# Sketched attention into a squared-ReLU network: the numerators of two groups by single heads on row halves of the TensorE array

## The chip, the core and the metric

The kernel runs on one core of a Trainium2 chip. The metric is the device time of one execution in microseconds; the number compared is the median over several executions. A profiled execution gives the trace, whose clock starts with the program's first instruction (its span).

## What is computed

Four batches with four heads each, 1088 tokens, 32 elements to a head. Queries and keys are sketched: two 8x32 matrices S1 and S2 are applied, and all 64 products of their results are the features. Each head's numerator and denominator come from one 64x33 state (64 features by 32 values and a column of ones). What all four heads give a token (128 numbers) goes through a two-layer network with a squared ReLU between the layers.

```python
def phi(x):
    a = np.einsum('rd,bhsd->bhsr', S1, x)
    b = np.einsum('rd,bhsd->bhsr', S2, x)
    return np.einsum('bhsi,bhsj->bhsij', a, b).reshape(*x.shape[:-1], r * r)
q_p, k_p = (phi(q), phi(k))
kv = np.einsum('bhsf,bhsd->bhfd', k_p, v)
z = np.sum(k_p, axis=2)
num = np.einsum('bhsf,bhfd->bhsd', q_p, kv)
den = np.einsum('bhsf,bhf->bhs', q_p, z)[..., None] + 1e-06
...
h = x @ w_in
r = np.maximum(h, 0.0)
g = r * r
return (g @ w_out).astype(np.float32)
```

## The kernel before

The program is a list of operations, recorded by `attention(b)` for four batches and `ffn(n, ...)` for nine stretches of 384 or 512 tokens. A table written out by hand, PLAN, gives the one order in which all of them are issued, the engine of each, and which buffer each takes. Nothing is reordered when it runs: each engine takes its instructions in that order and waits on semaphores. The result buffers in PSUM are three of two banks (h0, h1, h2), one bank a0 and one bank o0.

An entry such as `num3.0:PE:h1` is the numerator of batch 3, group 0, on TensorE into h1. For each batch the operations around the change are:

- `ksk`, `ka`, `kp` (L371, L376, L384): the features of the keys.
- `kv` (L400): the state of four heads, 72 pairs of weight load and matmul in the trace, contraction over 128 tokens, 64 columns of weights, 33 columns moved. Heads 0 and 2 write partitions 0 to 63 of one bank, heads 1 and 3 partitions 64 to 127.
- `kve` (L413): copies of the state into SBUF. `kvz[b]` is 128 x 2 x 2 x 33: for each pair of heads a block diagonal, head 0 of the pair in partitions 0 to 63 with zeros beside it, head 1 in partitions 64 to 127.
- `qp`: the features of the queries, 128 partitions (two heads of 64) x 2 pairs x 1088 tokens. In batches 0 and 1 TensorE makes them (L435) in products of 32 rows and 64 columns of weights, and VectorE multiplies (L452). In batches 2 and 3 they are read back through DRAM, and VectorE multiplies (L501).
- `num` (L535): the numerators. A group of up to 24 blocks of 32 tokens is `nx` times four blocks. For each of these, each pair of heads and each two blocks there is one float32 matmul: weights are 128 rows x 64 tokens of `qp`, and 66 columns of `kvz` move, so that a pair's two heads come out side by side and the zeros keep them apart. Batches 2 and 3 have two groups each: group 0 with nx = 6 (24 matmuls) into an h buffer, group 1 with nx = 3 into a0.
- `mxa` (L550 on ScalarE, L552 on VectorE): the denominators out of PSUM. `mx` (L557, L558): the reciprocal, and the quotient into `xs`, both VectorE.
- `tx` (L571) and `xe` (L576): transposes on TensorE, and the copy into xT, from which the network reads.

For the network, `m1.n.m` (L601) is two matmuls of 512 columns, `r` (L613 on ScalarE, L615 on VectorE) the ReLU out of h, `g` (L626, L628) the square of two of these, `m2` (L636) eight matmuls into o0, and `oe` (L643) the copy out. The h buffers turn over between `m1`, `r` and the attention: `num2.0` takes h0 after `r.3.0` on VectorE has read it. On TensorE the order around the two groups is `m1.2.7 num2.0 m1.3.7 m2.2.5 m2.2.6 m2.2.7 m1.3.2 tx2.0 kv3.0` and `num2.1 num3.0 tx2.1 m2.4.0 m1.5.0 m1.5.6`.

In the trace each float32 matmul shows as two records, each with its weight load.

Of the kernel before, what the change touches and what calls it, by code (L numbers as in the profile page):

```python
# [23 lines left out]
N_AA = 3  # L24
N_HEAT = 24
NUM_M = (64, 64, 64, 64)
W_PARTS = ((0, 1), (1, 2), (2, 4))
MODE = ('pe', 'pe', 'dma', 'dma')
Q_LOADS = (((0, 8), (8, 34)), ((0, 34),), ((0, 34),), ((0, 34),))
# [77 lines left out]
def kernel(  # L107
# [11 lines left out]
    nc = tc.nc  # L119
    B, H, S, D = q.shape  # L120
# [15 lines left out]
    def T(name, shape, dt=F32):  # L136
        return sb.tile(shape, dt, name=name, tag=name)
# [24 lines left out]
    def at(buf):  # L162
        return tiles[buf.slot]
# [23 lines left out]
    kvz = [T(f"kvz{i}", [128, 2, 2, D + 1]) for i in range(B)]  # L187
    kvs = [T(f"kvs{i}", [128, 2, 2, D + 1]) if MODE[i] == "pe" else None for i in range(B)]
    qp = [T(f"qp{i}", [128, 2, S]) for i in range(2)]
# [6 lines left out]
    def add(name, engines, fn, deps=(), alloc=(), uses=(), n=0, after=()):  # L196
        op = Op(name, engines, fn, deps, alloc, uses, n, after)
        ops.append(op)
        return op
# [5 lines left out]
    for x, src in ((0, S1), (1, S2)):  # L205
        def f(e, x=x, src=src):
            en = {"SP": nc.sync, "ACT": nc.scalar}[e]
            en.dma_start(out=S_sb[R * x : R * x + R, :], in_=src)
# [21 lines left out]
    def STx():  # L230
        return at(stb)[:, 0 : 2 * R].rearrange("p (x r) -> p x r", x=2)
    o_SK = add("SK", "DVE", lambda e: nc.vector.tensor_tensor(
        out=SK, in0=STx()[:, :, None, :].to_broadcast([128, 2, H, R]),
# [37 lines left out]
    o_gate = add("gate", "POOL", lambda e: nc.gpsimd.tensor_copy(gate, kin[0][:, S - 1 : S]), n=1)  # L271
    for lo, hi_ in W_PARTS:
        def f(e, lo=lo, hi_=hi_):
# [7 lines left out]
    def wpart(ct):  # L281
        return [i for i, (lo, hi_) in enumerate(W_PARTS) if lo <= ct // 4 < hi_][0]

# [6 lines left out]
    def attention(b):  # L290
        i = b % 2
# [3 lines left out]
        def mine(key, op):  # L295
            hist.setdefault((b, key), []).append(op)
            return op
# [210 lines left out]
        for g, (c0, c1) in enumerate(QG):  # L508
            nx = (c1 - c0 + 3) // 4
            pb = 2 if nx == 4 else 3  # L510
            nb, tb, db = Buf("h") if nx > 3 else Buf("a", "h"), Buf("a", "h"), Buf("den")

            def f_num(e, c0=c0, c1=c1, nx=nx, nb=nb, pb=pb):
                for x in range(nx):
                    lo = 512 * (x // pb) + 132 * (x % pb)
                    t = at(nb)[:, lo : lo + 132].rearrange(
                        "p (m d) -> p m d", d=33)
                    cs = []
                    for cc in range(4):
                        c = c0 + 4 * x + cc  # L520
                        c = c if c < c1 else c - 2
                        cs.append((c, mode == "pe" and 2 * (c - c0) >= c1 - c0))
                    runs = []
                    for cc, (c, sw) in enumerate(cs):
                        if runs and runs[-1][3] == sw and runs[-1][1] + runs[-1][2] == c:
                            runs[-1][2] += 1
                        else:
                            runs.append([cc, c, 1, sw])
                    if len(runs) > 1 or NUM_M[b] < 128:
                        two = all(cs[2 * z][0] + 1 == cs[2 * z + 1][0] and cs[2 * z][1] == cs[2 * z + 1][1] for z in range(2))  # L530
                        w = 2 if two and NUM_M[b] > 32 else 1
                        runs = [[cc, cs[cc][0], w, cs[cc][1]] for cc in range(0, 4, w)]
                    for pr in range(2):
                        for cc, c, w, sw in runs:
                            nc.tensor.matmul(  # L535
                                t[32 * cc : 32 * cc + 32 * w, 2 * pr : 2 * pr + 2, :],
                                qp[i][:, pr, 32 * c : 32 * c + 32 * w], (kvs if sw else kvz)[b][:, pr],
                                start=True, stop=True)
            o_num = mine("num", add(f"num{b}.{g}", "PE", f_num, o_qp[g] + o_kve, alloc=[nb], n=nx))

            def views(nx=nx, nb=nb, db=db, pb=pb):
                k_, m_ = (2, 4 * pb) if nx > 3 else (1, 4 * nx)
                t = at(nb).rearrange("p (b s) -> p b s", b=1 if nb.slot[0] == "a" else 2)[:, 0:k_, 0 : 33 * m_]
                return k_, m_, t.rearrange("p b (m d) -> p b m d", d=33), *at(db)

            def f_mxa(e, views=views):
                k_, m_, t, den, rec, xs = views()
                dd = den[:, 0 : k_ * m_].rearrange("p (b m) -> p b m", b=k_)
                if e == "ACT":
                    nc.scalar.activation(dd, t[:, :, :, D], ACTF.Copy, bias=eps)  # L550
                else:
                    nc.vector.tensor_scalar_add(dd, t[:, :, :, D], eps)  # L552
            o_mxa = add(f"mxa{b}.{g}", "DVE|ACT", f_mxa, [o_num], alloc=[db], uses=[nb], n=4 * nx)

            def f_mx(e, views=views, nx=nx):
                k_, m_, t, den, rec, xs = views()
                nc.vector.reciprocal(rec[:, 0 : k_ * m_], den[:, 0 : k_ * m_])  # L557
                nc.vector.tensor_tensor(  # L558
                    out=xs[:, 0:nx].rearrange("p (b x) (h d) -> p b (x h) d", b=k_, d=D), in0=t[:, :, :, 0:D],
                    in1=rec[:, 0 : k_ * m_].rearrange("p (b m) -> p b m", b=k_)[:, :, :, None].to_broadcast([128, k_, m_, D]),  # L560
                    op=ALU.mult)
            assert nx in (1, 2, 3, 4, 6)
            o_mx = add(f"mx{b}.{g}", "DVE", f_mx, [o_mxa], uses=[nb, db], n=nx)
            cols = 32 * (c1 - c0)

            def f_tx(e, tb=tb, db=db, cols=cols, nx=nx):
                t = at(tb).bitcast(BF16)
                xs = at(db)[2]
                for x in range(nx):
                    n = min(128, cols - 128 * x)  # L570
                    nc.tensor.transpose(t[:, 128 * x : 128 * x + n], xs[0:n, x, :], ident[0:n, 0:n])  # L571
            o_tx = add(f"tx{b}.{g}", "PE", f_tx, [o_mx, o_id], alloc=[tb], uses=[db], n=nx)

            def f_xe(e, t0=S * b + 32 * c0, tb=tb, cols=cols):
                fn = nc.scalar.copy if e == "ACT" else nc.vector.tensor_copy
                fn(xT[:, t0 : t0 + cols], at(tb).bitcast(BF16)[:, 0:cols])  # L576
            o_xe = add(f"xe{b}.{g}", "ACT|DVE", f_xe, [o_tx], uses=[tb], n=cols)
            x_ops.append((S * b + 32 * c0, S * b + 32 * c1, o_xe))
# [82 lines left out]
    for b in range(B):  # L661
        attention(b)
# [52 lines left out]
```

## Time and profile before

| what | us |
|---|---|
| runs shown | 118.04 and 119.79, median 118.92 |
| profiled execution | 116.81 |
| its span | 114.9 |
| TensorE busy | 107.0 (93%) |
| VectorE busy | 96.5 (84%) |
| ScalarE busy | 82.5 (72%) |

The profiled execution took 116.81 us, of which the span from the first to the last instruction is 114.9; the granted clock of TensorE is 0.999. A row of a timeline has the start and the length in microseconds, the engine (PE is TensorE's matmuls, PEld its weight loads, DVE VectorE, ACT ScalarE), the line, the operation with its tiles, the part of the array (rows*columns), shapes, and how many records were merged; in brackets stands the idle time before it. Matmuls overlap, so a merged row's length is from its first start to its last end.

### The profile page before, as it was taken

To read this page: it belongs to the slowest core of one execution; us is meant where nothing else is said; L and a number is where in the kernel's file an instruction comes from. 1 tells how busy PE (TensorE), PEld (TensorE's weight loads), DVE (VectorE), ACT (ScalarE), POOL (GpSimd) and SP (SyncE) were. 2 spreads that over 40 slices of the span, in tenths; PEclk is the share of its full clock that TensorE was granted. 3 is DMA by queue.
4 is the path that set the end of the run, shared out by engine and by line. 5 is a ranking of instruction groups with operands and counts; after the bars stand their busy time and mean duration, and the time that the engine had idled before them with its cause. 6 is when DMAs were issued, how large, how long until landed. Compare 5 with 4: busy or idle time off the path is not lost.

```text
span 114.9 us, 4029 instructions
## 1 busy us (share of the span) xinstructions
PE 107.0 (93%) x1716; PEld 77.4 (67%) x1716; DVE 96.5 (84%) x137; ACT 82.5 (72%) x114; POOL 10.5 (9%) x40
## 2 busy tenths in 40 slices
PE   5999997899999999999979999999999999999940
PEld 2346584667866766787768768877757877788730
DVE  1679998499596999999599689989999999999920
ACT  3134614285885899999992769998799798998910
POOL 4050540630000420000000000000000000000000
PEclk9999999999999999999999999999999999999999
DMA  2999899689699572376696126124200002022412
GB/s 60 323 296 239 269 321 183 122 229 195 169 261 232 142 218 108 83 164 156 148 176 141 41 71 183 34 69 140 82 0 13 10 6 69 0 67 72 115 38 59
DMA packets 10129, 15.23 MB, mean 133 GB/s; under 512 B 2112, under 2 KB 6976, under 8 KB 10112
## 3 DMA queue, kind: packets, MB, share of 16 engines
q1 hardware_dynamic: 8864, 13.80, 45.2%
q0 software_dynamic: 992, 1.05, 5.9%
q8 instruction: 13, 0.21, 0.8%
q10 hardware_dynamic: 256, 0.13, 0.5%
q14 instruction: 4, 0.03, 0.1%
HBM read 13.24 MB, written 2.79 MB: 139 GB/s over the span
## 4 chain that ended last, share of the span: by engine, by line
PE 75%; DVE 13%; ACT 4%; issue 3%; DVEq 0%; ACTq 0%
PE o L636 26%; PE h L601 25%; PE h L535 5%; PE o L263 4%; PE a L400 4%; DVE qp L452 3%; DVE qT L421 2%; DVE kp L384 2%; PE h L400 2%; PE h L435 2%; PE h L464 2%; PE a L535 2%; ACT r L613 1%; DVE xs L558 1%; PE h L371 1%
## 5 line engine op out<-in xcount | busy, mean ns | idle before, releaser
L613 ACT ACTIVATE r<-h 128x1024 bf16<-128x1024 f32 (+1 forms) x54 | 50.5, 979 | 8.9 <-PE h L601 7.9
L636 PEld LDWEIGHTS <-g 128*128 128x128 bf16 x544 | 32.6, 98 | 7.6 <-DVE g L628 1.5
L601 PE MATMUL h<-xT,w_in 128*128 128x512 bf16 (+1 forms) x144 | 37.1, 369 | 0.3
L636 PE MATMUL o<-w_out,g 128*128 128x128 bf16 x544 | 36.5, 219 | 0.1
L628 DVE TENSOR_TENSOR g<-r 128x2048 bf16<-128x2048 bf16 (+1 forms) x35 | 32.9, 969 | 0.8 <-ACT r L613 0.2
L615 DVE TENSOR_SCALAR r<-h 128x1024 bf16<-128x1024 f32 (+1 forms) x18 | 20.7, 1160 | 1.3 <-PE h L601 0.9
L601 PEld LDWEIGHTS <-w_in 128*128 128x128 bf16 x144 | 13.7, 115 | 6.0 <-issue 0.4
L626 ACT ACTIVATE g<-r 128x2048 bf16<-128x2048 bf16 (+1 forms) x9 | 14.0, 1556 | 0.7 <-DVE r L615 0.5
L447 ACT COPY A<-h 128x256 f32<-128x256 f32 (+2 forms) x12 | 5.0, 464 | 7.3 <-PE h L435 7.3
L263 PE MATMUL o<-zero 128*128 128x512 bf16 x24 | 8.1, 474 | 1.2 <-DVE zero L202 1.2
L384 DVE TENSOR_TENSOR kp<-a,ka 128x1280 f32<-128x1280 f32 (+1 forms) x5 | 6.9, 1370 | 0.0
L452 DVE TENSOR_TENSOR qp<-h,A 128x256 f32<-128x256 f32 (+2 forms) x12 | 6.0, 517 | 0.9 <-ACT A L447 0.8
L435 PE MATMUL h<-qT,SR 32*64 32x128 f32 (+2 forms) x192 | 6.2, 325 | 0.0
L535 PEld LDWEIGHTS h<-kvz,qp 128*64 128x64 f32 x136 | 4.4, 137 | 2.5 <-issue 1.1
L535 PE MATMUL h<-kvz,qp 128*64 128x66 f32 x136 | 5.0, 224 | 0.7 <-issue 0.6
L421 DVE STREAM_TRANSPOSE qT<-qin 128x1088 f32<-128x1088 f32 (+2 forms) x5 | 5.4, 1080 | 0.2 <-DMA qin<-in_q_dram 0.2
L435 PEld LDWEIGHTS h<-qT,SR 32*64 32x64 f32 x192 | 3.6, 131 | 2.6 <-issue 0.8
L643 ACT COPY osb<-o 128x512 f32<-128x512 f32 (+1 forms) x7 | 3.9, 561 | 1.9 <-PE o L636 1.8
L263 PEld LDWEIGHTS <-zero 128*128 128x128 bf16 x24 | 2.2, 110 | 4.4 <-issue 2.2
L501 DVE TENSOR_TENSOR qp<-qp,Bq 128x1536 f32<-128x1536 f32 (+1 forms) x4 | 5.1, 1283 | 0.0
L353 DVE STREAM_TRANSPOSE kT<-kin 128x1024 f32<-128x1024 f32 (+1 forms) x5 | 5.1, 1019 | 0.0
L400 PEld LDWEIGHTS a<-vp,kp 128*64 128x64 f32 x144 | 4.4, 138 | 0.9 <-issue 0.8
(69 smaller groups left out, 93.4 us busy)
## 6 DMA issues: line engine op xcount, KB each, us to landing
vin<-in_v_dram SPq DMA_DIRECT2D x16, 128.0 KB
out_dram<-osb SPq DMA_DIRECT2D x26, 64.0 KB
qin<-in_q_dram SPq DMA_DIRECT2D x3, 544.0 KB
kin<-in_k_dram SPq DMA_DIRECT2D x3, 544.0 KB
qp<-scr SPq DMA_DIRECT2D x4, 384.0 KB
Bq<-scr SPq DMA_DIRECT2D x8, 192.0 KB
qp<-scr SPq DMA_DIRECT2D x4, 160.0 KB
Bq<-scr SPq DMA_DIRECT2D x8, 80.0 KB
```

Source lines behind the costliest of these rows:

```text
L263: nc.tensor.matmul(at(heat_b), zero[:, 0:128], zero, start=True, stop=True)
L384: nc.vector.tensor_tensor(out=oo.rearrange("p (m x y) -> p m x y", x=R, y=R), in0=bb.rearrange("p (m y) -> p m y", y=R)[:, :, None, :].to_ ...
L400: nc.tensor.matmul(at(vb)[p : p + m, 33 * (h // 2) : 33 * (h // 2) + 33], kp[i][:, j, 64 * h + m * f : 64 * h + m * f + m], vp[i][:, h, j, :],
L435: nc.tensor.matmul(at(hb[h // 2])[lo : lo + 64, 512 * half + 256 * x : 512 * half + 256 * x + n], SR[32 * h : 32 * h + 32, x].rearrange("p ...
L452: nc.vector.tensor_tensor(out=qp[i][:, pr, t0 : t0 + 2 * n].rearrange("p (m s) -> p m s", m=2), in0=at(hb[pr]).rearrange("p (m s) -> p m s ...
L535: nc.tensor.matmul(t[32 * cc : 32 * cc + 32 * w, 2 * pr : 2 * pr + 2, :], qp[i][:, pr, 32 * c : 32 * c + 32 * w], (kvs if sw else kvz)[b][ ...
L601: nc.tensor.matmul(at(hb)[:, col(w) : col(w) + N], w_in[:, 512 * (ct // E) : 512 * (ct // E) + 512].rearrange("p (c e) -> p e c", e=E)[:, ...
L613: nc.scalar.activation(o, i_, ACTF.Relu)
L615: nc.vector.tensor_scalar_max(o, i_, 0.0)
L626: nc.scalar.activation(at(gb)[:, 0:tot], r, ACTF.Square)
L628: nc.vector.tensor_tensor(out=at(gb)[:, 0:tot], in0=r, in1=r, op=ALU.mult)
L636: nc.tensor.matmul(at(ob)[:, 128 * x : 128 * x + 128], at(gb)[:, lo + 128 * x : lo + 128 * x + 128], w_out[:, ct, :], start=(ct == 0 and x ...
```

## The change

A new table NUM_T names, for each batch, whether a group that lies in an h buffer is computed another way. It is empty for batches 0 and 1, "26" for batch 2 and "23" for batch 3. Groups in a0 keep the old way, so `num2.0` and `num3.0` alone change.

In these two groups a matmul computes one head instead of a pair. Its weights are the 64 rows of `qp` that belong to the head (partitions 0 to 63 or 64 to 127), and the 33 columns of the state of that head move; the zeros of `kvz` are not read. The first head of a pair writes the first bank of the h buffer, the second head the second bank, so the two row halves write different banks. With "26" the weights stay 64 tokens wide (24 matmuls become 48); with "23" they are 32 tokens wide (24 become 96). For x up to 2 the two heads alternate for each piece of tokens, from x = 3 on all pieces of the first head come before those of the second.

The views that `mxa` and `mx` read have the same 2 x 12 x 33 shape, and `mx` writes the same 768 elements to `xs` in pieces of 32, at steps that put the heads back in place. PLAN, the buffers, the copies of the state and the setting of its zeros are as before.

```diff
+NUM_T = ("", "", "26", "23")
...
-                    for pr in range(2):
-                        for cc, c, w, sw in runs:
+                    two_banks = NUM_T[b] and nb.slot[0] != "a"
+                    if two_banks and NUM_T[b][1] == "3":
+                        runs = [[cc, cs[cc][0], 1, cs[cc][1]] for cc in range(4)]
+                    todo = [(pr, r_, m) for pr in range(2) for r_ in runs for m in range(2)] if two_banks else [(pr, r_, None) for pr in range(2) for r_ in runs]
+                    if two_banks and x > 2:
+                        todo = [(pr, r_, m) for pr in range(2) for m in range(2) for r_ in runs]
+                    for pr, (cc, c, w, sw), m in todo:
+                        if not two_banks:
                             nc.tensor.matmul(
                                 t[32 * cc : 32 * cc + 32 * w, 2 * pr : 2 * pr + 2, :],
                                 qp[i][:, pr, 32 * c : 32 * c + 32 * w], (kvs if sw else kvz)[b][:, pr],
                                 start=True, stop=True)
+                            continue
+                        p = 64 * (m ^ int(sw))
+                        lo = 512 * m + 33 * (2 * x + pr)
+                        nc.tensor.matmul(at(nb)[32 * cc : 32 * cc + 32 * w, lo : lo + 33], qp[i][p : p + 64, pr, 32 * c : 32 * c + 32 * w], (kvs if sw else kvz)[b][p : p + 64, pr, m, :],
+                                         start=True, stop=True)
...
             def views(nx=nx, nb=nb, db=db, pb=pb):
+                if NUM_T[b] and nb.slot[0] != "a":
+                    t = at(nb).rearrange("p (b s) -> p b s", b=2)[:, :, 0 : 66 * nx]
+                    return 2, 2 * nx, t.rearrange("p b (m d) -> p b m d", d=33), *at(db)
...
-                    out=xs[:, 0:nx].rearrange("p (b x) (h d) -> p b (x h) d", b=k_, d=D), in0=t[:, :, :, 0:D],
+                    out=xs[:, 0:nx].rearrange("p x (r m d) -> p m (x r) d", r=2, m=2) if NUM_T[b] and nb.slot[0] != "a" else
+                    xs[:, 0:nx].rearrange("p (b x) (h d) -> p b (x h) d", b=k_, d=D), in0=t[:, :, :, 0:D],
```

TensorE's instructions around `num3.0`, before and then after (the row's end is the output's shape and the count):

```order
L601 MATMUL h_63<-xT,w_in 128x512
L535 MATMUL a_66<-kvz_130,qp_134 64x66 x12
L535 MATMUL h_64<-kvz_131,qp_135 64x66 x24
L571 LDWEIGHTS xs_83
L571 MATMUL a_66<-ident,xs_83 128x128
```

```order
L617 MATMUL h_63<-xT,w_in 128x512
L542 MATMUL a_66<-kvz_130,qp_134 64x66 x12
L549 MATMUL h_64<-kvz_131,qp_135 32x33 x96
L587 LDWEIGHTS xs_83
L587 MATMUL a_66<-ident,xs_83 128x128
```

Nothing moved: one row has become 96 smaller matmuls, between the same neighbours.

More of the change, by code (lines that the diff above doesn't have):

```diff
@@ L553, in attention, with f_mx @@
             o_mxa = add(f"mxa{b}.{g}", "DVE|ACT", f_mxa, [o_num], alloc=[db], uses=[nb], n=4 * nx)
-            def f_mx(e, views=views, nx=nx):
+            def f_mx(e, views=views, nx=nx, nb=nb):
                 k_, m_, t, den, rec, xs = views()
```

## The prediction

> **What bounds the kernel now.** I read the page first, then the chain of waits, then timelines of the two places that the change touches.
>
> ```profile
> span 114.9 us, 4029 instructions
> PE 107.0 (93%) x1716; PEld 77.4 (67%) x1716; DVE 96.5 (84%) x137; ACT 82.5 (72%) x114; POOL 10.5 (9%) x40
> ```
>
> TensorE is busy 93% of the span, VectorE 84%. The page alone doesn't say at which places a shorter numerator would help. The chain does it by place:
>
> ```profile
> 59.43 0.63 issue
> 60.06 1.63 PE h L535 x48
> 61.68 0.56 PE h L601 x2
> ...
> 76.69 1.40 PE h L535 x48
> 78.09 0.35 PE a L571 x3
> ...
> 82.99 0.68 DVE qp L501
> 83.67 1.15 DVE r L615
> ...
> 84.94 1.24 DVE g L628
> 86.22 1.07 PE o L636 x16
> ```
>
> The two L535 rows are `num2.0` and `num3.0`, 48 records each, 1.63 and 1.40 us, 3.0 us in all: more than that cannot be won. Both are on the chain. But ahead of the first stands an idle 0.63 us, and 5 us behind the second the chain leaves TensorE for VectorE and returns only at 86.22. The first place in detail:
>
> ```profile
> 58.74 1.22 DVE L615 TENSOR_SCALAR r<-h 128x1024 bf16<-128x1024 f32 x1
> 60.06 1.63 PE L535 MATMUL h<-kvz,qp 128*64 128x66 f32 x48 [0.63 <-issue]
> 60.09 2.36 DVE L628 TENSOR_TENSOR g<-r 128x2048 bf16<-128x2048 bf16 x2
> 61.72 0.19 ACT L550 ACTIVATE den<-h 128x24 f32<-128x24 f32 x1 [0.89 <-PE h L535]
> 62.37 0.29 DVE L557 RECIPROCAL rec<-den 128x24 f32<-128x24 f32 x1
> 62.77 0.96 DVE L558 TENSOR_TENSOR xs<-h,rec 128x768 bf16<-128x768 f32 x1
> 63.85 0.50 PE L571 MATMUL h<-ident,xs 128*128 128x128 bf16 x6
> ```
>
> `num2.0` starts 0.1 us after VectorE's ReLU at 58.74 has ended (59.96): it waits for h0, whatever the bracket calls it. Behind it ScalarE reads the denominators at once, but VectorE is busy with two squares until 62.45 and takes the reciprocal only then. The transposes at 63.85 need `xs`, which ends at 63.73. So a shorter `num2.0` would move TensorE forward by 0.12 us at most before it waits at these transposes; a longer one delays TensorE's next matmuls directly, while VectorE has 0.46 us to spare (den ends at 61.91, the reciprocal starts at 62.37). The second place:
>
> ```profile
> 76.52 1.57 PE L535 MATMUL h<-kvz,qp 128*64 128x66 f32 x48
> 77.68 1.22 DVE L615 TENSOR_SCALAR r<-h 128x1024 bf16<-128x1024 f32 x1
> 77.96 1.01 ACT L613 ACTIVATE r<-h 128x1024 bf16<-128x1024 f32 x1
> 78.03 0.42 PE L571 MATMUL a<-ident,xs 128*128 128x128 bf16 x3
> 78.86 0.18 ACT L550 ACTIVATE den<-h 128x24 f32<-128x24 f32 x1
> 78.95 1.02 PE L601 MATMUL h<-xT,w_in 128*128 128x512 bf16 x4
> 86.22 0.90 PEld L636 LDWEIGHTS <-g 128*128 128x128 bf16 x16 [0.59 <-DVE g L628]
> ```
>
> Here the denominators of `num3.0` wait behind a ReLU on ScalarE until 78.86, 0.77 us after the last numerator (78.09). The matmuls at 78.95 take h2, which VectorE's ReLU from 77.68 gives back at 78.90: TensorE can win 0.05 us there. A longer `num3.0` has cover as well: at 86.22 TensorE waits for a square that VectorE makes behind its own work, 0.59 us by the weight loads.
>
> **The change part by part.** What one record costs comes from three stretches of float32 records on parts of the array.
>
> ```profile
> 53.05 2.29 PE L400 MATMUL a<-vp,kp 128*64 128x33 f32 x72
> 5.49 0.69 PE L435 MATMUL h<-qT,SR 32*64 32x128 f32 x32
> 5.49 0.36 PE L435 MATMUL h<-qT,SR 32*64 32x128 f32 x8
> L435 PE MATMUL h<-qT,SR x192: 267/306/426, 5.5 to 22.5; 32*64 32x128 f32 x64, 32*64 32x256 f32 x64, 32*64 32x160 f32 x64
> L535 PE MATMUL h<-kvz,qp x136: 219/222/273, 20.4 to 77.9; 128*64 128x66 f32 x136
> L535 PEld LDWEIGHTS a<-kvz,qp x80: 106/137/139, 17.9 to 85.3; 128*64 128x64 f32 x72, 128*32 128x32 f32 x8
> ```
>
> (The third row is of a window from 5.49 to 5.64. Of the last three, the view of a line, only the durations in ns are used: least, median, most.) The last record of a stretch ends some 0.22 us after it starts, so `num3.0` runs at (1.57 - 0.22) / 47 = 28.7 ns a record, with 66 columns moved, and L400 at (2.29 - 0.22) / 71 = 29.2 ns with 33. **Half the columns, the same pace.** Two halves of the array's columns take turns in both, so each half accepts a record every 58 ns. In L400 33 columns cannot be what takes it; the load of 64 weight columns can: a load of 64 lasts 137 ns and one of 32 106 ns, 31 ns for 32 columns, so 62 for 64.
>
> L435 has eight parts, four row parts by two column halves, and its records of 128 columns end 0.27 us after their start, those of the first round 0.31 or more: (0.69 - 0.27) / 31 = 13.5 ns a record, 108 ns for each part with 128 columns moved (66 columns at 58 ns are the same 0.85 ns a column). Eight records start within the first 0.36 - 0.31 = 0.05 us, 7 ns apart. So **row parts do run beside each other**, and the pace is kept by each part, not by the engine, down to 7 ns.
>
> `num2.0`: 96 records on four parts, 24 rounds of four. A round costs what one part needs: the weight load of 64 columns, 58 ns; moving (33 x 0.85 = 28 ns) and issuing (4 x 7 = 28 ns) fit inside. 24 x 58 = 1.39 us, against 24 rounds of two at the same 58 before. **Change 0.00.** The bounds: if loads of 64 rows took half the time, a round is 28 ns and the gain 24 x 30 = 0.72 us, of which 0.12 can be used; if the two row halves took turns, a round is 117 ns and the loss 1.40. The row nearest to this form is L435's, so I take the first.
>
> `num3.0`: 192 records on eight parts, 24 rounds of eight. Issuing is 8 x 7 = 56 ns; the weight load of 32 columns is about 31, moving 28. 24 x 57 = 1.37: again 0.00. There is one thing new: the matmuls ahead of it (`num2.1`) use 128 rows by 64 columns, so the array's division changes between them, which it doesn't now. A change of division can be seen in batch 0:
>
> ```profile
> 25.68 0.63 PE L535 MATMUL a<-kvz,qp 128*64 128x66 f32 x9
> 26.07 0.26 PE L535 MATMUL a<-kvs,qp 128*32 128x66 f32 x3
> ...
> 37.47 0.45 PE L535 MATMUL h<-kvz,qp 128*64 128x66 f32 x8
> 37.76 0.40 PE L535 MATMUL h<-kvs,qp 128*64 128x66 f32 x8
> ```
>
> Eight records of 64 columns take 0.39 us to the next start where a 32-column form follows (the ninth in the row is its first), and 0.29 where the form stays: **0.10 us for a change of division**. So `num3.0` ends 0.1 us later. Its upper bound, a pace of 29 ns for every record whatever its part, is a rival below. This 0.1 us lies under the 0.59 us at 86.22.
>
> The two `xs` products write 32-element pieces at steps; the same 768 elements are read and written, 0.96 us each. I take 0; a tenth more would be 0.1 us, which at 62.77 shows as a later 63.85. The denominators' shapes, and every other instruction, stay as they are. Instructions: 48 and 144 more matmul records with as many loads are fetched; no row shows that TensorE ever ran out of them.
>
> Sum: 0.00 + 0.10 - 0.10 hidden = **no change**, 116.8 us for the profiled execution. The runs shown have a median 2.1 us above that profile, so **118.9 us**. A difference under 2%, 2.4 us, could not be told from no change.
>
> **The rivals.**
>
> *Each record takes its 29 ns, whatever its part* (the other side). For it: no row shows more than 32 records in a line below 28 ns, 64 instructions with their loads, and the numerators would need 96 and 192. Against it: in L435 records start 7 ns apart, and at 13.5 ns over all 32. Then `num2.0` takes 96 x 29 = 2.8 us (+1.4) and `num3.0` 192 x 29 = 5.6 us (+4.2), 0.1 for the division, less the 0.6 of cover at 86.22: +5.1 us, **124.0**. It decides from a pace of about 20 ns on: 96 x 20 = 1.9 (+0.5) and 192 x 20 = 3.8 (+2.5), and with the same two terms +2.5.
>
> The Trainium skill has a rule of this kind: "TensorE: Matmul & The Clock Gate", section "Wait — 56ns, not 53.3ns?", says that starts of matmuls never come closer than about 25 ns, however few columns move. By it the two groups would take 96 x 25 = 2.4 and 192 x 25 = 4.8 us, 4.4 us more, and with the same two terms the end would be near 122.8. The trace does not agree for records on different parts of the array: 7 ns and 13.5 ns in L435.
>
> *The row halves take turns* (the change doesn't do what it says). For it: no row of this trace has two row halves of 64. Against it: four row parts of 32 run beside each other in L435. Then `num2.0` loses 1.40 us; `num3.0` takes two loads of 32 columns (31 ns) a round, 62 instead of 57 ns, +0.1, and hides that. If the 0.59 us at 86.22 covered a part of the first, 119.7 were left; but VectorE's square there hangs on matmuls that would be late too, so **120.3.**
>
> *The row halves load in half the time.* `num2.0` takes 0.7 us less, but the transposes at 63.85 wait for VectorE, whose squares do not depend on it; `num3.0` is held by its issue. **118.8**: the gain goes into a wait for `xs`.
>
> **How the numbers follow.** Forecast 0.64, halves that take turns 0.14, faster loads 0.11, 29 ns a record 0.11. Only the last is over 2% slower. Of the faster cases none reaches 2% (2.4 us of the 3.0 would have to go, with VectorE in the way); I leave 0.03 for a drift of an order that is full on two engines, taken from the forecast. So faster 0.03, same 0.86, slower 0.11. The range: the two runs shown lie 0.9 us to either side of their median, so 117.4 below; above it takes in the halves that take turns with some of that scatter, 120.9. The 29 ns case stays outside.
>
> **What would show it.** In the profile after: `num2.0` with 96 records in 1.5 to 1.65 us, and `num3.0` with 192 records in 1.5 to 1.7; the L558 products of 768 elements still at 0.96 us; transposes of batch 2, group 0, right behind `xs`; TensorE still waiting for L628 near 86. A first row of 2.8 us would mean halves in turns; a second row over 2.5 us would break the 7 ns and bring the first rival.

## The result and the profile after

The changed kernel took 121.43 us (median of 2 runs, 120.98 to 121.87) against 118.92 before: a ratio of 1.033, interval 1.023 to 1.042. **It is slower by some 3%**; that it would take the same time had been forecast. The executions of one kernel fall into a fast and a slower state, and this ratio and all below compare fast ones alone, so they are not the ratios of the medians shown. The profiled executions, 116.81 us before and 120.98 after, differ by more than the medians: their spans are 114.9 and 119.0 us, and these 4.1 us are what has to be found.

The page of the changed kernel, with the lines that differ:

```profile
span 119.0 us, 4413 instructions
PE 110.0 (92%) x1908; PEld 79.8 (67%) x1908; DVE 96.8 (81%) x137; ACT 82.5 (69%) x114; POOL 10.5 (9%) x40
PEclk9999999999999999999999999997699999999999
q8 instruction: 15, 0.25, 0.9%
```

VectorE, ScalarE and GpSimd have the same instructions and the same work; TensorE has 192 matmuls and 192 weight loads more. Two lines are to be read twice. `PEclk` was nine everywhere before; now two slices between 80 and 86 us show 7 and 6. And q8, the queue that brings instructions from memory, has 15 packets of 16 KB where before had 13. With its 16 semaphore and drain instructions TensorE has 3832 instructions now (1908 matmuls, 1908 loads), 3448 before: 255 and 265 to a packet.

The chain of waits in the changed kernel, around the second group:

```profile
76.66 0.94 PE h L549 x59
77.59 0.00 issue
77.60 1.44 PE h L549 x51
79.04 1.59 issue
80.62 0.27 PE h L549 x9
80.89 0.35 PE a L587 x3
81.24 0.55 PE o L652 x8
81.80 1.58 PE h L617 x4
83.38 1.71 PE o L652 x16
```

L549 is the new numerator line. Before, this place read "76.69 1.40 PE h L535 x48", and then the transposes. Now there is a hole of 1.59 us in the middle of `num3.0`, put down to "issue": TensorE waits for nothing that the profile shows. (From the start of the last instruction ahead of it to the next one it is 1.80 us, and so are all standstills below counted.) Behind it 4 and 16 matmuls take 1.58 and 1.71 us; in before's chain the same rows took 0.97 and 0.89. The timeline of both groups on TensorE:

```profile
60.13 1.60 PE L549 MATMUL h<-kvz,qp 64*64 64x33 f32 x96 [0.62 <-issue]
...
75.73 0.92 PE L542 MATMUL a<-kvz,qp 128*64 128x66 f32 x24
76.58 2.45 PE L549 MATMUL h<-kvz,qp 64*32 64x33 f32 x183
80.62 0.27 PE L549 MATMUL h<-kvz,qp 64*32 64x33 f32 x9 [1.59 <-issue]
80.83 0.42 PE L587 MATMUL a<-ident,xs 128*128 128x128 bf16 x3
81.17 0.62 PE L652 MATMUL o<-w_out,g 128*128 128x128 bf16 x8
81.63 1.75 PE L617 MATMUL h<-xT,w_in 128*128 128x512 bf16 x4
83.17 1.91 PE L652 MATMUL o<-w_out,g 128*128 128x128 bf16 x16
```

`num2.0` is as short as forecast. `num3.0` lasts from 76.58 to the transposes at 80.83, 4.25 us instead of the 1.51 before (76.52 to 78.03). The busy time and clock of TensorE in the stretches behind (window, its length, busy time, instructions, granted clock, DMA share, GB/s):

```profile
76.59:80.83 4.24, 2.65 (x197) 1.00 0.48 141
80.83:81.80 0.97, 0.97 (x21) 1.00 0.52 178
81.80:85.21 3.41, 3.41 (x24) 0.50 0.00 0
85.21:89.00 3.79, 3.79 (x41) 1.00 0.00 0
```

The clock is 1.00 through the standstill and for 1.2 us behind it, then 0.50 for 3.41 us, then 1.00 again. Work at half rate for 3.41 us is 1.7 us lost.

The Trainium skill, "TensorE: Matmul & The Clock Gate", Part 1, describes a clock that is judged in windows of about 3.4 us and halved after at least one idle window. The trace agrees with the window, 3.41 us, and differs on the idle time: here a standstill of 1.80 us, half a window, was enough.

### The profile page after: what moved, and what is told of

It is laid out like the page before. It is cut to its first block, busy times and chain, and to the rows that moved or that the text cites. A ratio compares the mean times of both kernels' runs of the same rounds, so it can differ in the third digit from the quotient of the medians.

```text
span 119.0 us, 4413 instructions
## 1 busy us (share of the span) xinstructions
PE 110.0 (92%) x1908; PEld 79.8 (67%) x1908; DVE 96.8 (81%) x137; ACT 82.5 (69%) x114; POOL 10.5 (9%) x40
## 4 chain that ended last, share of the span: by engine, by line
PE 78%; DVE 11%; ACT 4%; issue 3%; ACTq 0%; DVEq 0%
PE o L652 26%; PE h L617 26%; PE o L264 4%; PE a L401 4%; PE h L549 4%; PE h L542 3%; DVE qp L453 2%; PE a L542 2%; PE h L436 2%; DVE qT L422 2%; DVE kp L385 2%; PE h L401 2%; PE h L465 2%; PE h L587 1%; ACT r L629 1%
## 5 line engine op out<-in xcount | busy, mean ns | idle before, releaser
L652 PEld LDWEIGHTS <-g 128*128 128x128 bf16 x544 | 33.6, 99 | 7.5 <-DVE g L644 0.6
L617 PE MATMUL h<-xT,w_in 128*128 128x512 bf16 (+1 forms) x144 | 37.8, 376 | 0.3
L652 PE MATMUL o<-w_out,g 128*128 128x128 bf16 x544 | 37.4, 222 | 0.0
L549 PE MATMUL h<-kvz,qp 64*32 64x33 f32 (+1 forms) x288 | 4.3, 208 | 2.2 <-issue 2.2
L549 PEld LDWEIGHTS h<-kvz,qp 64*32 64x32 f32 (+1 forms) x288 | 3.7, 115 | 3.1 <-issue 2.8
L572 DVE RECIPROCAL rec<-den 128x12 f32<-128x12 f32 (+3 forms) x10 | 2.3, 235 | 3.6 <-ACT den L565 3.2
```

What stands on the lines that cost most here:

```text
L549: nc.tensor.matmul(at(nb)[32 * cc : 32 * cc + 32 * w, lo : lo + 33], qp[i][p : p + 64, pr, 32 * c : 32 * c + 32 * w], (kvs if sw else kvz) ...
L617: nc.tensor.matmul(at(hb)[:, col(w) : col(w) + N], w_in[:, 512 * (ct // E) : 512 * (ct // E) + 512].rearrange("p (c e) -> p e c", e=E)[:, ...
L652: nc.tensor.matmul(at(ob)[:, 128 * x : 128 * x + 128], at(gb)[:, lo + 128 * x : lo + 128 * x + 128], w_out[:, ct, :], start=(ct == 0 and x ...
```

## The experiments

**The theories.** *A, instructions:* the standstill is TensorE out of instructions. They come in packets of 16 KB, taken here as 256 instructions; where a boundary between two packets falls into a dense group of short instructions, the next packet comes too late. Then the standstill must stay at one place in TensorE's instruction stream, and wander through `num3.0` when instructions are added ahead. *B, the form:* the 32-column parts with row halves themselves stall (a port, a queue of the array, the order of the parts). Then the standstill stays with `num3.0` wherever that stands in the stream. A side question was the pace of `num3.0` outside the standstill: its 192 records take 2.5 us, not 1.5.

For a comparison free of what comes earlier, "the stretch" below is the span less the start of `num2.0`: 114.9 - 60.06 = 54.8 us before, 119.0 - 60.13 = 58.9 after.

### Each half alone, a wider form, and a first shift

The table of forms, one entry per batch, in the first three: `e1_num2_alone`, `e2_num3_alone`, `e3_64_wide_both`.

```diff
-NUM_T = ("", "", "26", "23")
+NUM_T = ("", "", "26", "")      # e1
+NUM_T = ("", "", "", "23")      # e2
+NUM_T = ("", "", "26", "26")    # e3
```

The fourth keeps the change and cuts 22 of the 24 warming matmuls on zeros, at the start of the program, into 3 or 4 pieces: 64 matmuls and 64 loads more ahead of the groups, 128 instructions.

```diff
+HEAT_K = (4, 4, 4, 4, 4, 4, 4, 4, 4, 4, 4, 4, 4, 4, 4, 4, 4, 4, 4, 4, 3, 3, 1, 1)
...
-            nc.tensor.matmul(at(heat_b), zero[:, 0:128], zero, start=True, stop=True)
+            k = HEAT_K[i]
+            for c in range(k):
+                lo, hi = 512 * c // k, 512 * (c + 1) // k
+                nc.tensor.matmul(at(heat_b)[:, lo:hi], zero[:, 0:128], zero[:, lo:hi], start=True, stop=True)
```

What was expected:

> Only num2.0 keeps the new form (96 records of 64x64), num3.0 is as before. Theory A (instructions run out: in the changed kernel TensorE stood still for 1.8 us inside num3.0 while a 16 KB packet of the instruction queue was under way, and the clock was halved for 3.4 us afterwards): num2.0 takes 1.6 us as it did in the changed kernel, no standstill, no halved clock, time as before within 0.5 us. Theory B (row halves cost more by themselves, and the small records lower the clock): num2.0 costs a part of the loss too, +0.5 us or more.

> Only num3.0 keeps the new form (192 records of 64x32), num2.0 is as before, so TensorE has issued 96 instructions fewer when num3.0 starts. Theory A: the standstill comes at another record of num3.0 or not at all, since it stands at a fixed number of instructions; num3.0 between 1.8 us (no standstill) and 4.2 us. Theory B: num3.0 takes 4.2 us again and the whole 4 us of span are lost.

> Both groups with weights 64 tokens wide (96 records each, 4 parts). Theory A: 192 instructions in 1.5 us instead of 384 can be fed; num3.0 takes 1.5 to 1.7 us, clock 1.00, time as before within 0.5 us. Theory B: num3.0 loses too, in proportion to its records, about half of 2.7 us, and the clock is lowered.

> The changed kernel with 22 of the 24 warming matmuls at the start cut into 3 or 4 pieces of the same columns in sum: 128 more TensorE instructions early on, at the same array time, so every later instruction stands 128 places further on in the stream. Theory A (the standstill comes at a fixed place of the stream, once every 256 instructions at most): it moves by 128 instructions, out of num3.0's end, and num3.0 takes 1.8 to 2.6 us; the clock stays at 1.00; time within 1 us of before. Theory B (the loss belongs to the records of num3.0): num3.0 4.2 us as in the changed kernel, time as the changed kernel within 0.5 us.

Measured:

| run | median us | ratio to before (interval) | standstill in `num3.0` | stretch |
|---|---|---|---|---|
| e1, `num2.0` alone | 119.36 | 1.007 (0.997 to 1.018) | none | 54.7 |
| e2, `num3.0` alone | 118.51 | 1.008 (0.999 to 1.016) | none | 55.5 |
| e3, 64 wide in both | 117.82 | 1.001 (0.990 to 1.011) | none | 54.8 |
| e4, the change, +128 | 122.31 | 1.039 (1.028 to 1.051) | 1.38 us | 56.3 |

The half in batch 2 costs nothing measurable (e1). With 64-column parts in both batches the whole change costs nothing measurable (e3): here are the two groups in its chain of waits, 96 records each.

```profile
60.56 1.60 PE h L549 x96
...
77.09 1.53 PE h L549 x96
```

The 32-column form alone, 96 instructions earlier in the stream, does not stand still (e2); its row on the timeline is whole:

```profile
77.38 2.56 PE L549 MATMUL h<-kvz,qp 64*32 64x33 f32 x192
79.88 0.42 PE L587 MATMUL a<-ident,xs 128*128 128x128 bf16 x3
```

That speaks against B: the same form ran through. It takes 2.50 us to the transposes, 1 us more than before's 48 records, but the stretch grows by only 0.7 us (55.5 - 54.8).

e4 missed its expectation and is the best evidence so far. No standstill had been expected; there was one. Its timeline:

```profile
82.47 1.44 PE L553 MATMUL h<-kvz,qp 64*32 64x33 f32 x119
85.10 0.83 PE L553 MATMUL h<-kvz,qp 64*32 64x33 f32 x73 [1.19 <-issue]
```

In the changed kernel TensorE stopped with 183 of 192 records done (behind record 182, counted from 0); with 64 matmuls more ahead, with 119 done: **64 records earlier, and before the same instruction of the stream, TensorE's number 3009 in both traces** (matmuls, loads and its few semaphore instructions, counted from 0). The clock was not halved behind 1.38 us. Why e4 is slow all the same is told below.

### Out of the boundary, the order, and a shift by 32

`e5_shift_160` cuts the warming matmuls further (160 instructions), `e6_first_order` and `e7_second_order` are e5 with one order of the records throughout, and `e8_shift_32` shifts by 32.

```diff
+HEAT_K = (4, 4, 4, 4, 4, 4, 4, 4, 4, 4, 4, 4, 4, 4, 4, 4, 5, 5, 5, 5, 5, 5, 5, 5)  # e5, e6, e7
+HEAT_K = (1, 1, 1, 1, 1, 1, 1, 1, 2, 2, 2, 2, 2, 2, 2, 2, 2, 2, 2, 2, 2, 2, 2, 2)  # e8
-                    if two_banks and x > 2:
+                    if two_banks and x > 5:      # e6
+                    if two_banks:                # e7
```

> The changed kernel with the warming matmuls cut into 4 or 5 pieces: 160 more TensorE instructions early on. Theory A (a block of 256 instructions is asked for when TensorE's sequencer enters the block before it, and comes about 4 us later; in the changed kernel and with a shift of 128 the standstill came behind the same instruction of the stream, the 3009th record, 256 behind the last boundary): that boundary now falls 220 instructions into num3.0 less some, between its 90th and 115th record, and the boundary before it lies ahead of num2.1, so over 4 us pass between them. No standstill over 0.5 us; num3.0 2.3 to 2.7 us, as where it was changed alone; clock 0.995 or more; time +0.5 to +1.5 us against before. Theory B (num3.0's own records in company of num2.0's): standstill and halved clock stay, time 3 to 4 us over before.

> The same shift of 160, and in both groups the order of the first three steps kept for all six (the two row halves alternate). Theory A1 (the waits of 140 to 200 ns in the second half of num3.0 come from the second order): they vanish, and num3.0 takes 1.9 to 2.1 us. Theory A2 (they come from feeding, about every 100 instructions): they stay, num3.0 2.3 to 2.7 us.

> The same shift of 160, and in both groups the order of the last three steps for all six (four pieces of one row half, then four of the other). Theory A1: the waits of 140 to 200 ns stand in the first half of num3.0 too, which takes 2.7 us or more. Theory A2: as with the first order.

> The changed kernel with 16 warming matmuls cut into two: 32 more TensorE instructions early on. Theory A: the standstill stays behind the same instruction of the stream, so it comes 16 records earlier in num3.0 (after record 166 instead of 182), lasts 1.5 to 2.2 us, and the clock is halved afterwards; time as the changed kernel. Theory B (tied to a record of num3.0): after record 182 again.

e5 has no standstill in `num3.0` (2.49 us to the transposes), and a stretch of 55.4 us instead of 58.9. e8 has one of 1.83 us with 167 records done, 16 fewer than 183 and as expected, again before number 3009, and the clock is halved from 82.01, where it ends; the stretch is 59.0. Its timeline and its windows:

```profile
78.37 2.06 PE L553 MATMUL h<-kvz,qp 64*32 64x33 f32 x167
82.07 0.45 PE L553 MATMUL h<-kvz,qp 64*32 64x33 f32 x25 [1.64 <-issue]
```

```profile
82.01:85.42 3.41, 3.35 (x40) 0.50 0.23 73
85.50:89.00 3.50, 3.50 (x48) 1.00 0.00 0
```

The order of the records changes nothing: `num3.0` takes 2.45 us in e6 and in e7, 2.49 in e5, with the same small waits. One execution each: 121.63 (e6), 120.92 (e7), 122.84 us (e8).

But e5's time missed its expectation: 121.97 us, a ratio of 1.032 (1.018 to 1.047), no better than the change. The gain behind 60 us was lost ahead of it. The page of e5 and its timeline show where:

```profile
span 119.8 us, 4573 instructions
PEclk9999955589999999999999999999999999999999
```

```profile
10.57 1.25 PE L268 MATMUL o<-zero 128*128 128x128 bf16 x22
13.89 1.12 PE L268 MATMUL o<-zero 128*128 128x102 bf16 x17 [2.07 <-issue]
```

The warming matmuls, cut in five, are themselves dense short instructions: TensorE stands still between 11.61 and 13.89, and the clock is 0.50 from 14.53 to 24.77. `num2.0` starts at 64.43 instead of 60.13. So the cut was a poor tool: e4, e6 and e7 have such early standstills as well (the table of boundaries below), and the totals of e4 to e7 carry this; their stretches do not.

Another early loss is of a different kind. In e1, e4 and e7 to e11 TensorE waits 2.0 to 2.7 us near 30 us for `xs`, because VectorE waits for keys from memory; the traces of before and of the change don't have this wait. In e1, e4 and e10 a clock of 0.50 begins within 0.7 us of its end. It is another reason to go by the stretches.

### A cut that leaves the start alone

`e9_clean_shift` makes the same shift of 160 instructions elsewhere: 80 matmuls of the first MLP layer in the early groups are cut into two column halves, each still long. `e11_before_cut` is the kernel before with the same cut, and `e12_change_again` the change as it is; all of these ran on the same chip. `e10_32_wide_both` takes the 32-column form in batch 2 as well, which puts 192 instructions ahead.

```diff
-                    nc.tensor.matmul(
-                        at(hb)[:, col(w) : col(w) + N],
...
+                    split = n < 4 or (n == 4 and m < 6) or (n == 5 and m in (4, 5))
+                    for x0, x1 in ((0, X // 2), (X // 2, X)) if split else ((0, X),):
+                        nc.tensor.matmul(
+                            at(hb)[:, col(w) + 128 * x0 : col(w) + 128 * x1],
...
-NUM_T = ("", "", "26", "23")
+NUM_T = ("", "", "23", "23")    # e10, without the cut
```

> The changed kernel with the same shift of 160 instructions as e5_shift_160, but made by cutting 80 of the network's first-layer matmuls ahead of num3.0 into two halves of their columns, so that the warming at the start is untouched. Theory A: no standstill in num3.0, which takes 2.4 to 2.6 us, no halved clock after it; from the start of num2.0 to the end of the span 55.2 to 55.9 us (58.9 in the changed kernel, 54.8 before) plus what the cutting costs there, 0 to 0.5; time 0.5 to 1.5 us over before. Theory B: 58 us or more for that stretch.

> Both groups with weights 32 tokens wide: 192 records in num2.0 too, and num3.0 stands 192 instructions further on in the stream than in the changed kernel. Theory A: no boundary stands in num2.0 that was not asked for long before, so it has no standstill and takes 1.9 to 2.6 us; TensorE waits for a semaphore just ahead of num2.0 with nothing queued, so its first 32 records take 8 ns or more each, not 5.5 as in num3.0, where 64 instructions stood ready. The boundary after the one in num3.0 now lies some 40 instructions behind its end, and a standstill of 0.5 to 1.5 us comes there, in the transposes or the m2 and m1 matmuls that follow. Theory B: num2.0 takes 4 us as num3.0 did.

> The kernel before with the same 80 first-layer matmuls cut into two: what the cutting costs by itself. Theory A and B alike: 0 to +0.7 us, no standstill.

> The changed kernel itself on the same chip as e9_clean_shift, with nothing else altered. Theory A and B alike: standstill of 1.7 to 1.9 us behind record 182 of num3.0, halved clock for one window of 3.4 us after it, time 2.5 to 4.5 us over before.

| run | median us | ratio to before (interval) | standstill in `num3.0` | stretch |
|---|---|---|---|---|
| e9, the change, +160 by the cut | 119.22 | 1.015 (0.997 to 1.033) | none | 55.4 |
| e11, before with the cut | 119.21 | 1.016 (0.999 to 1.034) | (48 records) | 55.4 |
| e12, the change again | 122.21 | 1.044 (1.030 to 1.058) | 2.34 us | 59.5 |
| e10, 32 columns twice, one execution | 121.22 | | none | 55.9 |

**e9 and e11 are equal: without the standstill the change costs nothing measurable**, although its `num3.0` is longer. The cutting itself cost more than expected, by the ratio of e11 some 1.9 us instead of 0.7 at most; its trace holds the wait near 30 us. e12, with the standstill, is 3 us behind both; its standstill is longer than the 1.9 us expected. The timelines at `num3.0`, first e9, then e12:

```profile
78.25 2.29 PE L549 MATMUL h<-kvz,qp 64*32 64x33 f32 x192
80.48 0.42 PE L587 MATMUL a<-ident,xs 128*128 128x128 bf16 x3
```

```profile
77.63 2.46 PE L549 MATMUL h<-kvz,qp 64*32 64x33 f32 x183
82.22 0.34 PE L549 MATMUL h<-kvz,qp 64*32 64x33 f32 x9 [2.13 <-issue]
```

No variant was faster than before; the best, e3, equals it.

e10 missed in three points. The standstill expected behind `num3.0` did not come; the boundary was crossed only 2.5 us behind its end, after longer matmuls. In `num2.0` the 32-column form ran 192 records in 1.75 us (1.9 to 2.6 expected), where `num3.0` needs 2.48 for the same. And the first 32 of them started 5.4 ns apart, not 8 or more.

```profile
63.38 1.81 PE L549 MATMUL h<-kvz,qp 64*32 64x33 f32 x192 [0.62 <-issue]
...
80.03 2.55 PE L549 MATMUL h<-kvz,qp 64*32 64x33 f32 x192
```

### All boundaries of all traces

If A holds, it must hold for every boundary, so I numbered TensorE's instructions in each of the 14 traces, and set the instruction packets beside them. Boundaries stand 256 apart, at number 449, 705, and so on to 3009 and further (two or three lower in e9 to e12, whose traces lack three matmul records each): 190 in all, and one packet belongs to each in turn. At 174 TensorE passes with a gap of 0.25 us or less. At 16 it stands longer, 0.39 to 2.61 us, and **at each of the 16 it resumes 1.24 to 1.58 us after the end of that boundary's packet**:

| boundary | run: standstill, packet's end to resuming (us) |
|---|---|
| 449 | e2: 0.49, 1.36; e4: 0.52, 1.58; e5: 2.28, 1.55; e6: 0.88, 1.50; e7: 0.82, 1.34; e10: 0.39, 1.38; e12: 0.64, 1.45 |
| 705 | before: 0.59, 1.52; e3: 0.71, 1.40; e4: 2.41, 1.57; e6: 2.61, 1.42; e7: 1.66, 1.42 |
| 3009 | after: 1.80, 1.37; e4: 1.38, 1.33; e8: 1.83, 1.27; e12: 2.34, 1.24 |

In the changed kernel: packet from 78.30 to 79.25, the next instruction at 80.62. So A stands: place, wandering and packets agree, and B is excluded by e2, e5, e9 and e10, which ran the same form through. The table also holds the early standstills of e4 to e7; e4 and e7 lost time in the wait near 30 us besides.

How fast is too fast? At the late boundaries (beyond 2000) the 288 instructions up to and with the crossing never took less than 3.59 us. Where their own work took 3.65 us or more (e9 3.65, e10 3.78 and 4.03, e5 4.00, e2 4.02) there was no standstill; where it took less, TensorE stood for the rest (after 1.91 + 1.80 = 3.71; e8 3.59; e4 3.79; e12, whose packet took 1.62 us instead of 0.96, 4.25). At what moment a packet is asked for the traces don't show; 288 is a count fitted to these cases afterwards.

The Trainium skill, "Runtime: NRT & Kernel Launch", section "Instruction fetch mechanics", says that instructions are refilled in blocks of 16 KiB, 256 instructions, the next one while the current one runs, and that this is hidden because an engine issues more slowly than the blocks arrive. The traces agree with the block, and differ on the hiding: `num3.0` used up an instruction every 4.1 ns or so, and 16 of 190 boundaries were not hidden.

## Why the prediction was wrong

**The sum, as measured.** The stretches add up: 54.8 before; 55.4 to 55.5 with the small records and no standstill (e2, e5; +0.6); 58.9 with the standstill (1.80) and one window at half clock (1.7): 54.8 + 0.6 + 1.8 + 1.7 = 58.9. For e8, 55.4 + 1.8 + 1.7 = 58.9 (59.0 measured); for e12, 55.4 + 2.3 + 1.7 = 59.4 (59.5); for e4, without the halved clock, 55.4 + 1.4 = 56.8 (56.3). Ahead of `num2.0` nothing is lost.

**The step that failed** is the sentence "48 and 144 more matmul records with as many loads are fetched; no row shows that TensorE ever ran out of them". It was given no price, and the trace of before did hold such a row, in batch 0:

```profile
20.88 0.22 PE L535 MATMUL h<-kvs,qp 128*64 128x66 f32 x1
21.48 0.69 PE L535 MATMUL h<-kvs,qp 128*64 128x66 f32 x15 [0.37 <-issue]
```

One record, then 0.59 us of nothing in the middle of a group, put down to "issue". That is boundary 705, 1.52 us behind its packet. A count would have done the rest: 192 records are 384 instructions, so at least one boundary of 256 must fall into `num3.0`, and at the forecast pace (7 ns a record) 256 instructions last 0.9 us. In before the densest 256 took over 4 us. No rival named this, either: all of them were about the pace of a record. The outcome, 121.4, is outside the range, and beyond its upper end by 0.5 us. (The range's lower end doesn't follow from its reason: 118.9 less 0.9 is 118.0, not 117.4. Nothing hangs on it here.)

**`num2.0`**: right. 96 records in a row of 1.60 us ("1.5 to 1.65"), with four parts that run beside each other; the halves don't take turns, and nothing shows that loads of 64 rows are faster. The transposes behind still wait for `xs`, and the product is still 0.96 us. The changed kernel's timeline (PEld: weight loads):

```profile
62.84 0.96 DVE L573 TENSOR_TENSOR xs<-h,rec 128x768 bf16<-128x768 f32 x1
63.85 0.39 PEld L587 LDWEIGHTS <-xs 128*128 128x128 bf16 x6 [0.25 <-DVE xs L573]
63.91 0.50 PE L587 MATMUL h<-ident,xs 128*128 128x128 bf16 x6
```

**`num3.0`**: the term "issuing is 8 x 7 = 56 ns" was mis-sized. The first 32 records start 5.4 ns apart; then come about two in 16.5 ns, 8.3 ns a record, and four to six waits of 57 to 196 ns: 2.23 to 2.50 us without a standstill (e9, e2), where 1.37 and 0.1 had been forecast. The 7 ns came from eight records, too few to show a pace that lasts. The prediction's own test, "a second row over 2.5 us would break the 7 ns and bring the first rival", was met by 2.45 + 0.27 us, but not by that rival: 29 ns a record would be 5.6 us of steady work.

**The change of division**: right, 0.10 us. `num2.1` takes 0.85 us to the start of `num3.0` now (75.73 to 76.58), 0.75 before (75.77 to 76.52).

**The cover of 0.59 us at 86.22**: it hides a part of the longer `num3.0`, which is 1.0 us at the transposes and 0.6 to 0.7 at the end (e2, e5); beside e11 nothing is left of it (e9). Against 1.8 us and a halved clock it was no cover.

**What stays open:** what the waits of 57 to 196 ns in `num3.0` are. They don't depend on the order of the records (e6, e7), and `num2.0` of e10, the same form with other neighbours, lacks them. Also why the blocks at 449 and 705 were late at a slower pace than the late ones needed. That the standstill halves the clock, 1.7 of the 4.1 us, is argued from order and place alone (last section).

## What to carry to other kernels

Splitting work into more and shorter instructions has a price that no row of durations contains: count an engine's instructions in blocks of 256, and ask how long the shortest 288 in a row last; here TensorE stood still wherever the work up to a late boundary took less than some 3.6 us. A hole called "issue" in the middle of a uniform group is the mark of it, and its place in the stream, not in time, is to be compared: insert instructions ahead and see whether it wanders. When a shift is used as a tool, the inserted instructions must themselves be long, or they make the next hole.

## What the runs showed of the hardware

- An instruction packet of 16 KB (256 instructions) lasted 0.88 to 1.73 us in all cases but one (2.29, e2), and TensorE ran its first instruction 1.24 us after its end at the earliest where it was waiting for it.
- Of the 16 standstills, six of the seven of 1.66 us and more came with a clock of 0.50 that began between 0.8 us before TensorE resumed (e6) and 1.2 us behind (after), for 3.41 us in four (after, e7, e8, e12), 6.83 in e6 and 10.24 in e5; none of the nine from 0.39 to 1.38 us did. That the standstill is the cause is argued from this order alone; no run halted TensorE for that purpose.
- In all 14 traces the granted clock changes only at whole multiples of 3.413 us behind its first record (22, 23 and 33 of them in the changed kernel). Cut into such windows, ahead of 110 us all four with 1.65 us or more without a matmul were followed by a clock of 0.50 (e5 2.07, e12 1.91, e4 1.67, e10 1.65), five of the ten from 1.17 to 1.59 us (after 1.59, but e9 with 1.59 not), and none below among those at full clock. This fits e4's standstill of 2.41 us that lowered nothing: a window's end divides it, and leaves 1.22 and 0.82 us without a matmul on its two sides. Three of these nine drops (e1, e4, e10) came with the wait for `xs` near 30 us and not with a late packet.
- Matmuls of 64 rows by 32 columns on eight parts started 5.4 ns apart for 32 records, and 8.3 ns apart behind them, without the waits; 64 by 64 on four parts ran 96 in 1.53 us (e3), against 1.40 for 48 of 128 by 64 in before's chain.
